# Store and load queues in a Fourier-mixing plus gated-ReLU kernel: slice stores on ScalarE's queue, plain copies on GpSimd's, down weights loaded sooner in fewer transfers

## The chip, the cores and the metric

One core of a Trainium2 chip runs the whole kernel. The metric is the device time of one launch, in microseconds, as the median of several runs. One further execution is recorded by the hardware profiler; the stretches and waits below are from that one.

## What is computed

```python
S, D, F = 2048, 640, 1728
xn = layernorm(x)                                  # x: (1, S, D), eps 1e-5, no scale or bias
a  = einsum("bsd,ed->bse", xn, dft_hid_re)         # DFT along the hidden dimension
b  = einsum("bsd,ed->bse", xn, dft_hid_im)
y  = einsum("ts,bse->bte", dft_seq_re, a) - einsum("ts,bse->bte", dft_seq_im, b)
gate, up = xn @ W_gate, xn @ W_up                  # (D, F)
h  = gate * (gate > 0) * up
out = x + y + h @ W_down                           # (F, D)
```

All arrays are float32.

## The kernel before

Every float32 operand of a matmul is written as a high and a low part (`split`: ScalarE copies to the rounded type, L197, VectorE subtracts, L198), and each product is three matmuls (`mm3`, L203 to L205). On top of that the products are arranged in Strassen-like schemes, so that VectorE and GpSimd make sums of operand blocks and TensorE does fewer multiplications. The kernel has three stages.

**The sequence transform** (to about 410 us of the profile). The sequence is cut in four chunks of 512 columns. For each chunk, units named B11, B21, T1, T2, B22, T3, T4, each four groups long, load 512 KB blocks of the sequence matrices (`raw`, six buffers; `tk`, four buffers that live from T1 to T4), subtract blocks where the name begins with T (L743), split them, and multiply them with the normalized rows, which stay on chip. `drive(4, 2)` runs the list of units: at step i it first runs what was deferred to step i, then prepares unit i-2, loads unit i, finishes i-5, and multiplies i-4. Loads are issued by SyncE. In this stage the engines' orders are left to the framework's scheduler, but for the instructions that are pinned.

Into this list go four *slices* (`token_slice`): for 128 columns out of each chunk, the transposed input is loaded (L472, five transfers of 256 KB) with the rows of means and roots (L474, two), normalized on VectorE (L479), and combined in 28 sums (L488, L490) that the gate/up stage will use as operands. The normalized blocks and the sums are stored to `tok` in HBM (L495, at most 7 blocks a transfer, 7 transfers a slice). `SLICE_PLAN` gives for each slice the unit at which it begins, the units of its four normalizing steps, the units of its sums, and the unit of its last stores. All slices use one tile, `r`.

**The gate/up stage** (about 410 to 760 us). 13 tiles of gate and up weights go through a written-out order: an event has a key in units of one `mm3`, a tile starts every 33 units (`PERIOD`), and all events are sorted by key and issued so on all five engines (`manual_schedule(engines=PINNED)`). `STEPS` holds the multiplications, seeds, snapshots, additions and results ("final") of a tile; `WEIGHTS` its weight splits; `SUMS` the sums of weight blocks. `plan_sums` places those sums beside VectorE's own PSUM work on GpSimd (L992, `sum_beside`) and, where a sum's due time has come, on VectorE. The weights of tile n are loaded at 33 n - `LOAD_LEAD` (L979, L984, L989) into buffers that the tile two before it used. Results go to `hd` in HBM with `store_final` (L1123). Operands 0 to 13 of the combined ones are loaded into their own tiles, later ones into the slots of operands that are done (`fill_slot`, L832); `split_slot` splits them `SPLIT_LEAD` units before their use.

In the same order stand the *down-weight tasks*: five `quad_weights` and 24 `pair_half`, three a tile from the third tile on. Each loads blocks of the hidden or down matrix into one of two `pw` tiles (pool `prep`; L1288, L1251, L1252), makes sums on VectorE (`prepare`), rounds them on ScalarE and VectorE (`round_`, `rounded`, L1270, L1305), and stores them to `wparts` or `wquads` (L1274, L1276, L1308). `TASK_KEYS` gives the key of `prepare` and of `rounded` for each of the three. The parts that need no sums are copied from HBM to HBM by `plain_parts` (L1236, L1237; 12 calls of four transfers). `grow` makes accumulating copies on GpSimd's queue (L1334, L1335).

**The down projection** (from about 760 us) multiplies `hd` and the first stage's results `pq` with `wparts` and `wquads`. Its units load rows (`rw`) and weights (`wt`), and `prepare` splits both.

SyncE issues nearly all transfers, in order: a transfer whose buffer or data is not ready holds those behind it. ScalarE issues a few at the start and the end. GpSimd issues `grow`, results of the sequence transform (`pq`, `first`) and outputs.

Of the kernel before, what the change touches and what calls it, by code (L numbers as in the profile page):

```python
# [7 lines left out]
F32 = mybir.dt.float32  # L8
# [4 lines left out]
P = 128  # L13
S, D, F = 2048, 640, 1728
KD = D // P
# [84 lines left out]
UPPER_ORDER = (2, 3, 5, 6, 7, 11, 4, 1, 0, 8, 9, 10, 12, 13)  # L100
NEV, STORED = 12, 10
LATE_LOW = 2
LEAD_ORDER = (2, 3, 5, 6, 7, 1, 0, 11, 8, 9, 10, 4, 13, 12, 5, 6)
LEADS = ((12, (24, 26)), (22, (34, 36)), (29, (40,)), (38, (45, 47)), (46.5, (52,)))
LEAD_SLOTS = (36, 37, 40, 41, 44, 45, 47, 49, 50, 51, 54, 55, 56, 57, 58, 59, 60, 61, 63, 64, 65, 66, 67, 68)
SPLIT_LEAD, FIRST_SPLIT = 6.5, -20
TASK_KEYS = ((5.2, 7.4), (14.6, 18.4), (29.7, 32.7))
LOAD_LEAD, LOADED = 48, 38
SLICE = P
# [16 lines left out]
def fnet_reglu_kernel(  # L126
# [329 lines left out]
    def token_slice(s):  # L456
# [9 lines left out]

        def load():
            if "work" not in late:
                late["work"] = get_r1(F32)
            t["w"] = late["work"]  # L470
            for k in range(KD):
                nc.sync.dma_start(by_chunk(at(k * NT, NT)), by_chunk(xt[k * P : (k + 1) * P])[:, :, cs])  # L472
            for i in range(2):
                nc.sync.dma_start(by_chunk(at(WORK_MR + i * NT, NT)), by_chunk(rows[i : i + 1])[:, :, cs].to_broadcast([P, NT, SLICE]))  # L474

# [15 lines left out]

        def store(first, at_, n):
            for i in range(0, n, 7):
                k = min(7, n - i)
                nc.sync.dma_start(tok[first + i : first + i + k, :, cs].rearrange("i p t -> p i t"), at(at_ + i, k).rearrange("p (i t) -> p i t", i=k))  # L495

        def begin():
            load()
            here, norms, units, end = SLICE_PLAN[s]
            for i, (k0, k1) in enumerate(((0, 2), (2, KD))):  # L500
                for m in range(2):
                    defer(norms[2 * i + m] - here, lambda m=m, k0=k0, k1=k1: normal(m, k0, k1))
            defer(norms[-1] + 1 - here, lambda: store(0, 0, NX))
            for i, part in enumerate(TOKEN_SUMS):
                defer(units[i * len(units) // len(TOKEN_SUMS)] - here, lambda part=part: sums(*part))
            defer(end - here, lambda: store(NX, WORK_OUT, NCOMBO))

# [374 lines left out]

    SLICE_PLAN = ((22, (26, 28, 29, 30), (30, 32, 33, 34, 39), 40), (40, (46, 48, 49, 50), (51, 53, 55, 56, 57), 58), (58, (67, 68, 69, 70), (72, 74, 77, 78), 79), (80, (88, 89, 90, 91), (93, 95, 98, 99), 100))
    SLICE_UNITS = [begin for begin, *_ in SLICE_PLAN]

# [113 lines left out]
    def plan_sums():  # L999
# [9 lines left out]
        def due_at(i):  # L1009
            if i not in due:  # L1010
                o = SUMS[i][1]
                raw = max(SUMS[i][3:]) >= ZR
                due[i] = min([split_at.get(o, 99.0) - 11, 2 * PERIOD - LOAD_LEAD - 1.0 if raw else 99.0] + [due_at(j) - 0.8 for j in reads.get(o, ())])
            return due[i]
# [117 lines left out]
    for n in range(NF):  # L1132
        k0 = PERIOD * n
        at(k0 - LOAD_LEAD if n > 1 else -70 + n * 30, load_tile, n)
        for key, *what in SUMS if n < 2 else ():
            at(max(k0 + key, 5 + key / 20) if n == 1 else k0 + key, sum_step, n, *what)
        for g, what in enumerate(WEIGHTS):
            at(k0 + what[0], high, n, g)
            at(k0 + what[0] + SPLIT_AHEAD, low, n, g)
        for key, what, *args in STEPS:  # L1140
            at(k0 + key, DO[what], n, *args)
            if what == "final":
                at(k0 + key + 2.2, store_final, n, args[0])

# [86 lines left out]
    def plain_parts(k):  # L1231

        wa, wb = pair(k, 1)
        for w, o1, o in ((wa[0], Y11, O1), (wb[0], Y12, O2)):
            rows = slice(0, w.shape[0])
            nc.sync.dma_start(wparts[rows, k, o1 : o1 + 2 * P], w[:, : 2 * P])  # L1236
            nc.sync.dma_start(wparts[rows, k, o : o + P], w[:, 2 * P : 3 * P])  # L1237

    def pair_half(k, h):
# [6 lines left out]
        def load():  # L1246
            t["z"] = z = pool("prep").tile([P, 12 * P], F32, name="pw")
            wa, wb = pair(k, 1)
            for w, o1, o2 in ((wa[0], y11, y21), (wb[0], y12, y22)):
                rows = slice(0, w.shape[0])  # L1250
                nc.sync.dma_start(z[rows, o1], w[:, h * P : (h + 1) * P])  # L1251
                nc.sync.dma_start(z[rows, o2], w[:, (3 + h) * P : (4 + h) * P])  # L1252

# [60 lines left out]
    for i, (load, prepare, round_, rounded, store) in enumerate(tasks):  # L1314
        key, second = (PERIOD * (2 + i // len(TASK_KEYS)) + key for key in TASK_KEYS[i % len(TASK_KEYS)])
        at(key - 7, load)
        at(key, prepare)
        at(key + 1.2, round_)
        at(second, rounded)
        at(second + 1.5, store)  # L1320
    for k in range(NPAIR):
        at(30 + 8 * k, plain_parts, k)

# [126 lines left out]
    def project(q):  # L1450
# [27 lines left out]
        def unit(name, u, first, last):  # L1478
# [42 lines left out]
            def prepare():  # L1521
# [18 lines left out]
                with in_turn():  # L1540
# [19 lines left out]
                    t["b"] = b = pool("ring2").tile([P, 2, SG, CH], F32R, name="cb")[:, :, :n]  # L1560
                    lows.append(split(b[:, 0], b[:, 1], src))
                    if name not in PARTS:
                        w = t["w"]
                        split(w[:, :, 0], w[:, :, 1], w[:, :, 1].bitcast(F32))

# [215 lines left out]
```

## Time and profile before

| | us |
|---|---|
| median of 3 runs | 1036.5 (1036.24 to 1039.34) |
| profiled execution, device time | 1042.62 |
| its span, first to last instruction | 1040.8 |
| TensorE busy | 1008.0 (97%) |
| VectorE busy | 886.1 (85%) |
| ScalarE busy | 526.7 (51%) |
| GpSimd busy | 120.5 (12%) |

The page gives busy time by engine, the span in slices, DMA queues, the chain of work that ended last, groups of instructions, and DMA issues. In its rows PE is TensorE's matmuls, PEld its weight loads, DVE VectorE, ACT ScalarE, POOL GpSimd and SP SyncE; a q behind an engine's name is its queue. `raw<-in_dft` is what an instruction writes and reads, buffer numbers left out; L743 is a line of the kernel. Sequencer work such as issuing a DMA is not counted as busy. A wait is put down to the event that ended it.

### The profile page before, as it was taken

Reading aid. Unit: us, or ns where it says so; the run is one execution under the profiler, and the core shown is the slowest. Engines: PE = TensorE matmul, PEld = TensorE weight load, DVE = VectorE, ACT = ScalarE, POOL = GpSimd, SP = SyncE. Lnnn points to the kernel's source line nnn. Section 1 sums busy time; section 2 is a strip of 40 time slices with the busy share of each in tenths; the row PEclk is TensorE's granted clock in tenths of the full one; section 3 lists DMA queues with packets and bytes.
Section 4 is the critical chain, followed back from the end, with each engine's and each line's share of the span. In section 5 each row is a group of like instructions: output and inputs, shape, how many; then the busy total and the mean of one; then the engine's idle time right before and its main releaser. Section 6 shows DMA issues by size and latency. Waiting matters only on the chain.

```text
span 1040.8 us, 13595 instructions
## 1 busy us (share of the span) xinstructions
PE 1008.0 (97%) x4393; PEld 825.4 (79%) x4393; DVE 886.1 (85%) x1442; ACT 526.7 (51%) x832; POOL 120.5 (12%) x235
## 2 busy tenths in 40 slices
PE   9999999899999999999899989999999999999998
PEld 8888888688788888777778768778878888888887
DVE  7969999888889989997889879897878888599887
ACT  6654443223233555675566556666534554454552
POOL 2000000000000000022323323322000000000001
PEclk9999999999999999999899999999999999999999
DMA  9887895965958858749867978753689688999685
GB/s 333 327 252 241 278 316 180 365 205 191 345 181 298 318 182 257 270 140 255 243 197 218 213 210 228 208 167 120 199 331 359 215 260 296 321 314 346 209 273 178
DMA packets 189319, 261.14 MB, mean 251 GB/s; under 512 B 15712, under 2 KB 133984, under 8 KB 189152
## 3 DMA queue, kind: packets, MB, share of 16 engines
q1 hardware_dynamic: 179776, 226.03, 65.6%
q0 software_dynamic: 9040, 33.82, 10.9%
q8 instruction: 34, 0.56, 0.2%
q10 hardware_dynamic: 432, 0.43, 0.1%
q14 instruction: 37, 0.30, 0.1%
HBM read 198.34 MB, written 75.94 MB: 264 GB/s over the span
## 4 chain that ended last, share of the span: by engine, by line
PE 62%; DVE 20%; DMA 10%; ACT 3%; issue 3%; SPq 2%; POOL 0%; DVEq 0%; ACTq 0%; POOLq 0%
PE ps L203 19%; PE ps L204 19%; PE ps L205 19%; DVE cb L198 4%; PE ps L576 3%; DMA wparts<-pw 2%; DMA tk<-in_dft 2%; DVE raw L743 2%; DMA hd<-ev 1%; DMA pw<-in_wd 1%; DVE ev L1102 1%; DVE r L490 1%; DVE gw L992 1%; DMA pw<-in_hid 1%; DVE tk L743 1%
## 5 line engine op out<-in xcount | busy, mean ns | idle before, releaser
L203 PE MATMUL ps<-cb,wt 128*128 128x512 f32 (+1 forms) x389 | 151.5, 389 | 1.2 <-ACT cb L197 1.2
L204 PE MATMUL ps<-cb,wt 128*128 128x512 f32 (+1 forms) x389 | 151.8, 390 | 0.8 <-DVE cb L198 0.8
L205 PE MATMUL ps<-cb,wt 128*128 128x512 f32 (+1 forms) x389 | 151.4, 389 | 0.0
L197 ACT ACTIVATE cb<-rw 128x1024 fp32r<-128x1024 f32 (+1 forms) x91 | 86.5, 962 | 79.5 <-PE ps L205 40.6
L197 ACT ACTIVATE cb<-raw 128x1024 fp32r<-128x1024 f32 x64 | 67.8, 1061 | 106.9 <-PE ps L205 76.5
L198 DVE TENSOR_TENSOR cb<-rw,cb 128x1024 fp32r<-128x1024 f32 (+1 forms) x91 | 99.5, 1104 | 21.4 <-ACT cb L197 20.8
L204 PE MATMUL ps<-cb,xs_late 128*128 128x512 f32 x232 | 92.4, 398 | 7.7 <-DVE cb L198 7.7
L1087 ACT ACTIVATE ps<-ps 128x512 f32<-128x512 f32 x104 | 60.2, 582 | 71.4 <-DVE ps L1097 43.3
L205 PE MATMUL ps<-cb,xs_late 128*128 128x512 f32 x232 | 91.8, 396 | 0.0
L198 DVE TENSOR_TENSOR cb<-raw,cb 128x1024 fp32r<-128x1024 f32 x64 | 77.9, 1220 | 16.3 <-ACT cb L197 16.0
L203 PE MATMUL ps<-cb,xs_late 128*128 128x512 f32 x232 | 91.5, 394 | 0.0
L204 PE MATMUL ps<-cb,xs_early 128*128 128x512 f32 x226 | 88.3, 391 | 0.0
L203 PE MATMUL ps<-cb,xs_early 128*128 128x512 f32 x226 | 88.2, 390 | 0.0
L205 PE MATMUL ps<-cb,xs_early 128*128 128x512 f32 x226 | 88.2, 390 | 0.0
L203 PEld LDWEIGHTS ps<-cb,wt 128*128 128x128 f32 x389 | 73.4, 189 | 16.8 <-ACT cb L197 1.6
L204 PEld LDWEIGHTS ps<-cb,wt 128*128 128x128 f32 x389 | 73.4, 189 | 16.1 <-DVE cb L198 1.1
L205 PEld LDWEIGHTS ps<-cb,wt 128*128 128x128 f32 x389 | 73.5, 189 | 15.2
L194 ACT ACTIVATE ev<-ps 128x512 f32<-128x512 f32 x117 | 68.8, 593 | 24.7 <-PE ps L205 22.1
L1102 DVE TENSOR_TENSOR ev<-ps,ev 128x512 f32<-128x512 f32 x91 | 62.3, 685 | 9.2 <-PE ps L205 8.8
L197 ACT ACTIVATE wt<-wt 128x768 fp32r<-128x768 f32 (+5 forms) x60 | 38.4, 645 | 53.7 <-DMA wt<-wparts 50.1
L197 ACT ACTIVATE cb<-tk 128x1024 fp32r<-128x1024 f32 x32 | 33.9, 1061 | 61.0 <-PE ps L205 27.3
L203 PE MATMUL ps<-mv,w 128*128 128x512 f32 x143 | 57.2, 400 | 7.7 <-ACT ps L1087 7.6
(248 smaller groups left out, 2283.8 us busy)
## 6 DMA issues: line engine op xcount, KB each, us to landing
raw<-in_dft SPq DMA_DIRECT2D x94, 512.0 KB, 6.3
wt<-wparts SPq DMA_DIRECT2D x74, 256.0 KB, 4.7
rw<-hd SPq DMA_DIRECT2D x27, 512.0 KB, 6.2
hd<-ev SPq DMA_DIRECT2D x45, 256.0 KB, 3.6
tok<-r SPq DMA_DIRECT2D x24, 448.0 KB, 5.1
wt<-wparts SPq DMA_DIRECT2D x27, 384.0 KB, 4.3
rw<-pq SPq DMA_DIRECT2D x19, 512.0 KB, 5.7
wparts<-pw SPq DMA_DIRECT2D x24, 384.0 KB, 3.5
```

What stands on the lines that cost most here:

```text
L194: return nc.scalar.activation(o, i, AF.Copy)
L197: nc.scalar.activation(hi, src, AF.Copy)
L198: return nc.vector.tensor_tensor(lo, src, hi.bitcast(F32), op=OP.subtract)
L203: nc.tensor.matmul(ps, wh, mh, start=first, stop=False, skip_group_check=more)
L204: nc.tensor.matmul(ps, wh, ml, start=False, stop=False, skip_group_check=more)
L205: nc.tensor.matmul(ps, wl, mh, start=False, stop=last, skip_group_check=more)
L490: pin(tt(two(o[0], o[3]), two(o[1], o[4]), two(o[2], o[5]), op=op))
L576: nc.tensor.matmul(E[0, key], xn_part(n * SG + j, d)[v == 1], b[:, int(v == 2), j], start=False, stop=n % NH == NH - 1 and (j, v) == (SG - ...
L743: sub = lambda o, i0, i1: nc.vector.tensor_tensor(o, i0, i1, op=OP.subtract)
L992: return (engine or nc.vector).tensor_tensor(operand(n, o), operand(n, a), operand(n, b), op=OP.add if op == "+" else OP.subtract)
L1087: nc.scalar.activation(banks[n, x], banks[n, s], AF.Copy, scale=float(sign))
L1102: tt(t, banks[n, x], snaps[n, s], op=OP.add if op == "+" else OP.subtract)
```

## The change

- Slice stores (L495) are issued by ScalarE instead of SyncE, and each of the three or four transfers has a step of its own. A slice's seven loads are spread over steps 0 to 4 behind its begin (`SLICE_LOADS`), its last stores over 1 and 2 steps behind the planned end (`SLICE_STORES`). `SLICE_PLAN` is new; slice 2 begins at 62 instead of 58, slice 3 at 81 instead of 80.
- The plain copies are issued by GpSimd, one every 6 units from key 66 on, instead of four at a time every 8 units from key 30 on by SyncE.
- A down-weight task's load comes 9.5 units before `prepare` instead of 7, its store 3 units after `rounded` instead of 1.5; `pair_half` loads in two transfers instead of four; `TASK_KEYS` is new.
- A gate/up tile is loaded 46 instead of 48 units ahead, and sums of raw blocks are due at 11.5 instead of 17.
- A result's store comes 4 units after it instead of 2.2 (and its buffer counts as used for 11 instead of 10); operand splits come 5.5 units before their use instead of 6.5, and the first at -16 instead of -20.
- In the down projection, T1's weight split of the first half is issued after the ScalarE copy of the last B11 rows.

```diff
-NEV, STORED = 12, 10
+NEV, STORED, STORE_LAG = 12, 11, 4
...
-SPLIT_LEAD, FIRST_SPLIT = 6.5, -20
-TASK_KEYS = ((5.2, 7.4), (14.6, 18.4), (29.7, 32.7))
-LOAD_LEAD, LOADED = 48, 38
+SPLIT_LEAD, FIRST_SPLIT = 5.5, -16
+TASK_LEAD, TASK_KEYS = 9.5, ((8.2, 12.4), (14.6, 18.4), (28.0, 29.9))
+LOAD_LEAD, LOADED, RAW_DUE = 46, 38, 11.5
+SLICE_LOADS, SLICE_STORES = (0, 1, 2, 3, 3, 4, 4), (1, 1, 2, 2)
...
-        def store(first, at_, n):
-            for i in range(0, n, 7):
-                k = min(7, n - i)
-                nc.sync.dma_start(tok[first + i : first + i + k, :, cs].rearrange("i p t -> p i t"), at(at_ + i, k).rearrange("p (i t) -> p i t", i=k))
+        def store(first, at_, i, n):
+            k = min(7, n - i)
+            nc.scalar.dma_start(tok[first + i : first + i + k, :, cs].rearrange("i p t -> p i t"), at(at_ + i, k).rearrange("p (i t) -> p i t", i=k))
 
         def begin():
-            load()
             here, norms, units, end = SLICE_PLAN[s]
+            for unit, f in zip(SLICE_LOADS, [lambda k=k: load(k) for k in range(2)] + [lambda i=i: load_rows(i) for i in range(2)] + [lambda k=k: load(k) for k in range(2, KD)]):
+                if unit:
+                    defer(unit, f)
+                else:
+                    f()
...
-            defer(norms[-1] + 1 - here, lambda: store(0, 0, NX))
+            for i in range(0, NX, 7):
+                defer(norms[-1] + 1 + i // 7 - here, lambda i=i: store(0, 0, i, NX))
...
-            defer(end - here, lambda: store(NX, WORK_OUT, NCOMBO))
+            for i in range(0, NCOMBO, 7):
+                defer(end + SLICE_STORES[i // 7] - here, lambda i=i: store(NX, WORK_OUT, i, NCOMBO))
...
-    SLICE_PLAN = ((22, (26, 28, 29, 30), (30, 32, 33, 34, 39), 40), (40, (46, 48, 49, 50), (51, 53, 55, 56, 57), 58), (58, (67, 68, 69, 70), (72, 74, 77, 78), 79), (80, (88, 89, 90, 91), (93, 95, 98, 99), 100))
+    SLICE_PLAN = ((22, (26, 28, 28, 29), (30, 33, 33, 35, 39), 40), (40, (46, 49, 50, 52), (52, 53, 55, 55, 57), 58), (62, (66, 67, 69, 70), (72, 74, 77, 77), 81), (81, (88, 89, 90, 93), (93, 95, 98, 99), 100))
...
-                due[i] = min([split_at.get(o, 99.0) - 11, 2 * PERIOD - LOAD_LEAD - 1.0 if raw else 99.0] + [due_at(j) - 0.8 for j in reads.get(o, ())])
+                due[i] = min([split_at.get(o, 99.0) - 11, RAW_DUE if raw else 99.0] + [due_at(j) - 0.8 for j in reads.get(o, ())])
...
-                at(k0 + key + 2.2, store_final, n, args[0])
+                at(k0 + key + STORE_LAG, store_final, n, args[0])
...
-        for w, o1, o in ((wa[0], Y11, O1), (wb[0], Y12, O2)):
-            rows = slice(0, w.shape[0])
-            nc.sync.dma_start(wparts[rows, k, o1 : o1 + 2 * P], w[:, : 2 * P])
-            nc.sync.dma_start(wparts[rows, k, o : o + P], w[:, 2 * P : 3 * P])
+        return [lambda w=w, o=o, c=c: nc.gpsimd.dma_start(wparts[: w.shape[0], k, o : o + (c.stop - c.start)], w[:, c])
+                for w, o1, o in ((wa[0], Y11, O1), (wb[0], Y12, O2)) for o, c in ((o1, slice(0, 2 * P)), (o, slice(2 * P, 3 * P)))]
...
-            for w, o1, o2 in ((wa[0], y11, y21), (wb[0], y12, y22)):
-                rows = slice(0, w.shape[0])
-                nc.sync.dma_start(z[rows, o1], w[:, h * P : (h + 1) * P])
-                nc.sync.dma_start(z[rows, o2], w[:, (3 + h) * P : (4 + h) * P])
+            blocks = z.rearrange("p (o n) -> p o n", n=P)
+            for w, put in ((wa[0], slice(2, 5, 2)), (wb[0], slice(3, 11, 7))):
+                nc.sync.dma_start(blocks[: w.shape[0], put], w.rearrange("p (o n) -> p o n", n=P)[:, h : h + 4 : 3])
...
-        at(key - 7, load)
+        at(key - TASK_LEAD, load)
...
-        at(second + 1.5, store)
-    for k in range(NPAIR):
-        at(30 + 8 * k, plain_parts, k)
+        at(second + 3, store)
+    for i, f in enumerate(f for k in range(NPAIR) for f in plain_parts(k)):
+        at(2 * PERIOD + 6 * i, f)
...
+                    if name == "B11":
+                        late["copied"] = next(i for i in reversed(nc.cur_bb.bb.instructions) if i.engine == mybir.EngineType.Activation)
                     if name not in PARTS:
                         w = t["w"]
-                        split(w[:, :, 0], w[:, :, 1], w[:, :, 1].bitcast(F32))
+                        with tc.issue_after(late["copied"]) if (q, name) == (1, "T1") else ExitStack():
+                            split(w[:, :, 0], w[:, :, 1], w[:, :, 1].bitcast(F32))
```

More of the change, by code (lines that the diff above doesn't have):

```diff
@@ L465, in at, with load @@
             return t["w"][:, o * SLICE : (o + n) * SLICE]
-        def load():
+        def load(k):
             if "work" not in late:
@@ L470, in load, with load_rows @@
             t["w"] = late["work"]
[L471 to L474, printed above, removed]
+            nc.sync.dma_start(by_chunk(at(k * NT, NT)), by_chunk(xt[k * P : (k + 1) * P])[:, :, cs])
+        def load_rows(i):
+            nc.sync.dma_start(by_chunk(at(WORK_MR + i * NT, NT)), by_chunk(rows[i : i + 1])[:, :, cs].to_broadcast([P, NT, SLICE]))
         def normal(m, k0, k1):
```

## The prediction

> **What bounds the kernel now.** I read the page's first part, then the table of stretches, TensorE's waits, and for each stretch that loses time the queue or the chain of work in it. TensorE is the bound: it is busy for 97% of the span, so what can be gained is where it stands still, and the half clock that follows.
>
> ```profile
> span 1040.8 us, 13595 instructions
> 200.00:212.00 12.00, 6.82 (x18) 5.04 (x17) 9.04 (x10) 3.17 (x3) 0.14 (x1) 0.72 0.99 397
> 212.00:273.00 61.00, 61.00 (x271) 50.46 (x270) 53.05 (x64) 19.91 (x20) 2.55 (x5) 1.00 0.67 218
> 273.00:281.00 8.00, 5.46 (x18) 4.10 (x17) 6.71 (x6) 1.46 (x2) 0.00 (x0) 0.79 1.03 420
> 412.00:490.00 78.00, 74.65 (x321) 59.21 (x320) 70.75 (x161) 54.03 (x107) 14.79 (x30) 1.00 0.72 219
> 490.00:530.00 40.00, 33.40 (x133) 26.36 (x132) 29.01 (x67) 20.69 (x42) 9.16 (x18) 0.91 0.84 249
> 570.00:615.00 45.00, 38.53 (x160) 30.39 (x159) 35.03 (x82) 25.55 (x52) 14.74 (x27) 0.96 0.90 222
> 615.00:665.00 50.00, 49.88 (x219) 40.63 (x218) 45.00 (x103) 31.76 (x63) 17.70 (x36) 1.00 0.78 212
> 665.00:710.00 45.00, 43.51 (x190) 34.99 (x189) 40.45 (x97) 28.75 (x58) 11.93 (x25) 1.00 0.57 167
> 760.00:769.00 9.00, 7.03 (x24) 5.16 (x23) 6.55 (x7) 3.99 (x5) 0.54 (x1) 0.81 0.98 362
> 769.00:1025.00 256.00, 256.00 (x1131) 211.97 (x1130) 213.17 (x252) 121.81 (x157) 8.47 (x16) 1.00 0.87 293
> ```
>
> Behind each stretch stand its length, then busy time and count of TensorE, weight loads, VectorE, ScalarE and GpSimd, the granted clock, the DMA engines' busy share and GB/s. The last row is TensorE undisturbed: 256.00 us for 1131 matmuls, 0.2263 us each. Length minus count times 0.2263 is what a stretch loses:
>
> - A, 200 to 212: 7.9 us. B, 273 to 281: 3.9. Both in the sequence transform.
> - C, 412 to 490, where the gate/up stage starts: 5.4.
> - D, 490 to 530: 9.9; 570 to 615: 8.8; 615 to 665: 0.4; 665 to 710: 2.0; together 21.1, inside the gate/up stage.
> - E, 760 to 769, at the start of the down projection: 3.6.
>
> In all 42.0 us, clock loss included (in A, 12 us at 0.72 lose 3.4 to the clock alone). 615 to 665 says more: there VectorE and ScalarE do the whole of their gate/up work, and TensorE runs at full rate. So D is no lack of VectorE, it is lateness.
>
> Why A and B are late, from SyncE's queue, VectorE and the chain of work in order of time (start, length, what):
>
> ```profile
> 177.87 3.80 SPq L495 DMA_DIRECT2D tok<-r  x4
> 181.71 4.14 SPq L472 DMA_DIRECT2D r<-in_xt  x4
> 185.90 2.30 SPq L474 DMA_DIRECT2D r<-rows  x2
> 185.77 2.35 DVE L743 TENSOR_TENSOR raw<-raw,tk 128x1024 f32<-128x1024 f32 x2
> 191.58 11.58 DMA tk<-in_dft
> 203.25 1.23 DVE L743 TENSOR_TENSOR tk<-tk,raw 128x1024 f32<-128x1024 f32 x1 [2.50 <-DMA tk<-in_dft]
> PE ps L204 <- DVE cb L198: 8.5, 3, 5.2
> 251.50 4.55 SPq L495 DMA_DIRECT2D tok<-r  x4
> 256.09 4.67 SPq L472 DMA_DIRECT2D r<-in_xt  x4
> 265.19 9.00 DMA tk<-in_dft
> ```
>
> From 177.87 to 188.20 SyncE's queue does nothing but store one slice's sums (L495) and load the next slice (L472, L474). The matrix tile that T1 of the next chunk needs (tk) could have been asked for at 188.12, when the two L743 subtractions that free its buffers are done; it is asked for at 191.58, behind other late loads, and takes 11.58 us. VectorE stops in front of its subtraction, the low half that TensorE wants next stands behind that in VectorE's order, and TensorE idles 5.2 us. B is the same picture one chunk later.
>
> Why D is late, from SyncE's waits in the gate/up stage, its queue there, and the chain:
>
> ```profile
> SPq L984 <- DVE gw L992: 28.3, 6, 6.4
> SPq L1276 <- DVE pw L1270: 21.0, 16, 3.0
> SPq L979 <- DVE gw L992: 15.9, 4, 5.4
> SPq L1251 <- DMA wparts<-pw: 14.4, 12, 4.1
> 583.25 0.35 SPq L984 DMA_DIRECT2D gw<-in_wgu  x1
> 587.28 5.36 DMA pw<-in_hid
> 596.29 6.61 DMA wparts<-pw
> wparts<-pw SPq DMA_DIRECT2D x24, 384.0 KB, 3.5
> L1236 SPq DMA_DIRECT2D wparts<-in_wd x14: 496/605/1636, 468.2 to 513.3; - x14
> 483.66 8.44 DMA wparts<-in_wd
> ```
>
> (Total us, times, longest.) One queue carries everything: the gate/up tile load waits until a VectorE sum has read the old tile (L984, L979), the down-weight store waits for its rounding (L1276), the next down-weight load waits for a buffer (L1251). Loads of pw stand behind all of these, so they land as VectorE reaches their prepare step, or later: at 587.28 the load takes 5.36 us more, and VectorE, in order, holds up the sums on which ScalarE's seeds and TensorE hang. At 483.66 the plain copies wparts<-in_wd add 8.44 us in front of a pw load.
>
> **The change part by part.** One unit of the gate/up order is three matmuls, 0.68 us.
>
> *Slice stores on ScalarE, slice transfers spread (A, B).* The 28 stores leave SyncE; slice 2 begins at unit 62 instead of 58, its seven transfers at 62 to 66 instead of all at once, stores one or two units after the sums. In A, tk's second load can then go at 188.12, 3.5 us sooner, and four of the seven transfers (256 KB each) go behind it, at 397 GB/s another 2.6 us: landing near 197.1 instead of 203.16. TensorE needs 5.2 us, so the idle time goes; VectorE has no slack there, so I leave 0.8 us. A: -7.1. In B the slice begins at 81 instead of 80 and its stores move from 79 to 82 and 83, so the same bytes still meet T1's loads. tk is again freed earlier than it is asked for, but I count only half of the 2.5 us of idle time as gone, with the clock loss (8 us at 0.79, 1.7 us): 1.4 remain. B: -2.5.
>
> What the stores cost on ScalarE:
>
> ```profile
> L495 SPq DMA_DIRECT2D tok<-r x28: 365/512/2040, 100.7 to 322.9; - x28
> SPq L495 <- DVE r L479: 34.3, 8, 8.8
> L197 ACT ACTIVATE cb<-raw 128x1024 fp32r<-128x1024 f32 x64 | 67.8, 1061 | 106.9 <-PE ps L205 76.5
> ```
>
> The issues take 512 ns in the median (365 to 2040), 14 us for 28, on an engine that is busy 19.91 us of 61 and whose high-half copies (cb<-raw) wait 76.5 us for TensorE to free a buffer. I take +0.5, between 0 and what the third rival says.
>
> *Gate/up loads and down weights (D).* The raw sums' due time goes from 17.0 (2 x 33 - 48 - 1) to 11.5, and the tile load from key 18 to 20; walking the planner's rule through with both, one raw sum of each tile moves, and it stays on VectorE. So the load no longer finds its buffer read late. The rounding's store comes 3 units after it, not 1.5; a final's store 4 after it, not 2.2. The down-weight load leads by 9.5 units instead of 7, in two transfers instead of four. The third task of a tile: its load stood behind the tile load and the second task's store (VectorE's key 18.4); with about 2 us of issue and 5.36 us to land it came at key 29.4, wanted at 29.7. Now it is keyed 18.5, ahead of both, and waits only for the first task's store: rounding at 12.4, 3.5 us to land by the row of its kind (to key 17.6 to 18.5, counting issue), then 3 to 5.4 us: key 23 to 26.5, wanted at 28.0. That is 1 to 3 us of slack in place of none. The 48 plain copies leave SyncE (0.6 us each in front of pw loads) and go one per 6 units. I take 70% of D away: -14.8; the rest covers landings like the 6.61 us above and late seeds, which stay.
>
> ```profile
> L1334 POOL DMA_DIRECT2D grown<-grown x6 | 3.3, 547 | 5.2 <-DMA grown<-hd 4.8 <-DMA grown<-pq 0.4
> DVE gw L992 <- POOL gw L992: 2.2, 3, 1.8
> ```
>
> The copies cost GpSimd 48 x 0.55 = 26 us, on an engine with two thirds of its time free (14.74 of 45 busy). What can be late is its sums: VectorE waited 2.2 us for them beside 24 such DMAs. Twice as many: 4.4 at most, 0 at least; I take +1.5, between the two and nearer to the row's own 2.2.
>
> *Start of the gate/up stage (C).* Splits move 4 and 1 units later, giving VectorE room first and less lead after. The trace has no row for either; 0, plus or minus 2.
>
> *The order at the down projection (E).* T1's weight split is held behind ScalarE's copy of B11.
>
> ```profile
> 758.48 3.33 DMA wt<-wparts
> 761.90 0.84 ACT L197 ACTIVATE wt<-wt 128x768 fp32r<-128x768 f32 x1 [7.32 <-DMA wt<-wparts]
> 762.65 1.99 ACT L197 ACTIVATE cb<-rw 128x1024 fp32r<-128x1024 f32 x2
> ```
>
> ScalarE sat idle 7.32 us for T1's weights and only then copied B11's rows, for which TensorE was waiting. With the copies first, E goes but for about 0.7: -2.9 (0 if their buffers are not free sooner).
>
> Sum: -7.1 - 2.5 + 0.5 - 14.8 + 1.5 - 2.9 = -25.3 on the profiled execution, whose own time is 1042.6 (span 1040.8): 1017.3. The median of the runs, 1036.5, is 6.1 shorter. I take it that those 6.1 are of the same stalls, so scale by (42.0 - 6.1)/42.0 = 0.855: -21.6, 1014.9.
>
> **The rivals.**
>
> 1. *The DMA engines, not the queue, are full.* At 200 to 212 they are 0.99 busy, at 273 to 281 1.03. If the same bytes land as late, A and B stay: -25.3 + 9.6 = -15.7, times 0.855 is -13.4, 1023. Against it: 212 to 273 ran at 0.67, so there is room before B, and in A the queue stood waiting for VectorE first. The Trainium skill, "DMA: Bandwidth & Descriptors", section "Issuing engines are not separate DMA queues", says that DMAs of all issuing engines run on the same 16 engines and that another issuer saves sequencer time only; by that rule it is this rival that holds. The trace agrees inside A (397 GB/s), and shows with L495's 34.3 us of waits that a queue can hold transfers back for another reason.
> 2. *The down-weight buffers hold the queue.* There are two; a store that comes 1.5 units later frees its buffer later, and the third load, keyed 18.5, waits on SyncE in front of the tile load. If D gives a third (-7.0): -17.5, times 0.855 is -15.0, 1021.5. With the first rival too: 1030.
> 3. *ScalarE stops for the slices* (the other side). SyncE stood 34.3 us for L479 in front of L495. If ScalarE stands as long, each time with a cb copy behind it that TensorE wants, that is up to +34.3, less the 0.5 already counted, some 1049. It decides from 21.6, two thirds of those waits: from there the kernel is slower. Against it: SyncE runs ahead of VectorE and ScalarE does not, since its copies wait for VectorE's subtractions or TensorE's buffers, and the store comes a unit after its data.
> 4. *No change*, each stall replaced by the next late thing: 1036.
>
> **How the numbers follow.** Forecast 52% (its own spread about 1005 to 1021), rival 1 18%, rival 2 19%, both 2%, rival 3 6%, no change 3%. 0.3%, 3.1 us, is about what a measurement can tell. Faster 0.91, same 0.03, slower 0.06. Low end: all of A, B, D and E (36.5 times 0.855 is 31.2) and 2 of C, 1003; I stop at 1004. High end: both rivals, 1030.
>
> **What the changed profile would show.** Right: no wait for cb of over 2 us near 200 and 273, tk landing within 8 us of its issue; no half clock between 490 and 615; L984 and L979 waits below 10 us in sum; ScalarE copying cb before its third wt at the down projection. Wrong: ScalarE waiting for r before L197 (rival 3), SyncE's wait for wparts<-pw above 14.4 us (rival 2), tk still 9 to 12 us on its way (rival 1), VectorE waiting for GpSimd's sums by more than 5 us, or new gaps at C.

## The result, and the profile after

The changed kernel is faster, by about half to four fifths of the forecast gain.

| | changed, us | before, us | ratio, 95% interval |
|---|---|---|---|
| first comparison | 1026.27 (1024.63 to 1026.56, 4 runs) | 1037.05 (1036.24 to 1039.34) | 0.9889 [0.987, 0.9909] |
| second comparison, another chip | 1024.49 (1024.26 to 1025.15, 4 runs) | 1042.08 (1039.99 to 1045.72, 11 runs) | 0.983 [0.9813, 0.9848] |

The two intervals do not meet. Between them the changed kernel moved by 1.8 us and the kernel before by 5.0; in the other two groups of runs below the kernel before stood at 1041.19 and 1040.56. So the gain is 10.8 us or 17.6, and most of the difference is in the kernel before. What makes the kernel before vary so was not found. The profiled executions were 1042.6 before (span 1040.8), 1026.4 and 1024.3 after (spans 1024.6 and 1022.5).

The table of stretches, first of the kernel before and then of the changed one. The borders are the starts of TensorE's matmuls number 800, 1100, 1300, 1800, 2100, 2600, 3100 and 3500 (of 4393), so each pair of rows is the same work; the third row of each, 500 undisturbed matmuls, is left out. The columns are length, TensorE's busy time (count), granted clock, busy share of the DMA engines, GB/s.

```profile
177.54:254.04 76.50, 71.32 (x301) 0.96 0.73 249
254.04:303.84 49.80, 47.26 (x201) 0.97 0.88 309
...
417.17:490.77 73.60, 70.25 (x301) 1.00 0.71 212
490.77:624.04 133.27, 120.20 (x501) 0.96 0.79 221
624.04:740.45 116.41, 114.81 (x501) 1.00 0.62 179
740.45:835.78 95.33, 93.07 (x401) 0.98 0.82 286
```

```profile
177.70:250.32 72.62, 70.14 (x301) 0.98 0.78 264
250.32:298.55 48.23, 46.18 (x201) 1.00 0.84 308
...
411.88:484.33 72.45, 70.27 (x301) 1.00 0.60 183
484.33:608.66 124.33, 115.95 (x501) 1.00 0.87 246
608.66:725.37 116.71, 115.34 (x501) 1.00 0.65 188
725.37:819.53 94.16, 92.50 (x401) 1.00 0.84 289
```

A, the first row, is 3.9 us shorter, B 1.6, C 1.2, D (two rows) 249.7 to 241.0, 8.6, and E 1.2. At 0.2263 us a matmul the lengths would be 67.9, 45.3, 67.9, 226.3 and 90.5: A still loses 4.7 us, D 14.7.

**What is left in A**, from the changed kernel. The stores of a slice (L495) between 177 and 207 (issue ns min/median/max, first and last start):

```profile
L495 ACTq DMA_DIRECT2D tok<-r x4: 366/370/521, 177.9 to 185.1; - x4
DMA to landing us min/median/max: 5.0/9.1/20.0
```

SyncE's queue by the timeline (start, length, line), the landing of the four `tk` loads between 180 and 212, the waits of SyncE and TensorE, and the last step of the chain of work:

```profile
177.91 1.25 SPq L472 DMA_DIRECT2D r<-in_xt  x2
179.20 3.15 SPq L475 DMA_DIRECT2D r<-rows  x2
182.40 1.93 SPq L472 DMA_DIRECT2D r<-in_xt  x2
...
187.05 1.46 SPq L753 DMA_DIRECT2D tk<-in_dft  x2
...
194.06 11.46 SPq L753 DMA_DIRECT2D raw<-in_dft  x2
205.60 0.38 SPq L753 DMA_DIRECT2D tk<-in_dft  x1
```

```profile
DMA to landing us min/median/max: 4.8/10.9/11.1
```

```profile
SPq L753 <- DMA tok<-r: 12.8, 4, 10.5
PE ps L205 <- DVE cb L199: 2.5, 1, 2.5
```

```profile
205.60 4.84 DMA tk<-in_dft
```

The store issued at 185.1 lands after 20.0 us, at 205.1, and until then SyncE stands in front of a load: 10.5 us, the 11.46 of its two issues. That load does not touch `r`. By the trace's semaphore events the transfers of SyncE and ScalarE take turns on eight completion semaphores, and an issue waits until the earlier transfer on its semaphore has landed; this load's was the store's. Only then is the fourth tk asked for (205.60); it lands quickly (4.84), but late, and TensorE idles 2.5 us. So the stores left SyncE's queue and still hold it. The first lines show a second thing: with no store in front of them, six of the slice's seven loads (the first went at 169.94) are issued in one go from 177.91 to 184.3, all of them before the first tk (187.05). The spread of the loads is gone from the queue, and three of the four tk loads take 10.7 to 11.1 us.

**What is left in D**: SyncE's waits, those of VectorE, TensorE and GpSimd, and two pieces of the chain.

```profile
SPq L1255 <- DMA wparts<-pw: 69.4, 24, 5.9
SPq L1291 <- DMA wquads<-pw: 10.5, 3, 5.5
SPq L985 <- DVE wb L1074: 7.5, 2, 7.1
SPq L990 <- DVE gw L998: 3.3, 1, 3.3
PE ps L204 <- DVE ev L1108: 8.0, 5, 3.2
DVE gw L998 <- POOL gw L998: 6.5, 5, 3.0
POOL grown L1337 <- DMA grown<-hd: 7.4, 1, 7.4
```

```profile
483.84 7.76 DMA wquads<-pw
492.05 5.72 DMA pw<-in_wd
...
580.49 9.93 DMA grown<-hd
590.76 4.07 DMA grown<-grown
```

The waits that D was made of before, of tile loads for a sum (`gw`), are down from 44.2 us to 3.3; a wait for a weight split (`wb`) is 7.5, before 3.7. In their place SyncE waits 69.4 us (51.6 in the second profile) for down-weight stores to land, since a task's load needs the tile that the store still reads. At 483.84 a store takes 7.76 us, the next load goes at 492.05 and takes 5.72, and TensorE stands 3.2 us near 497. The second piece is GpSimd's queue: an accumulating copy (`grown<-hd`) takes 9.93 us to land, and GpSimd waits 7.4 us of them before it issues the copy of its result (`grown<-grown`, 4.07), for which the next accumulating copy waits in turn. GpSimd's sums stand behind, and VectorE (6.5 us) behind them.

### The profile page after: what moved, and what is told of

It is laid out like the page before. It is cut to its first block, busy times and chain, and to the rows that moved or that the text cites. A ratio compares the mean times of both kernels' runs of the same rounds, so it can differ in the third digit from the quotient of the medians.

```text
span 1024.6 us, 13553 instructions
## 1 busy us (share of the span) xinstructions
PE 1001.7 (98%) x4393; PEld 817.9 (80%) x4393; DVE 884.8 (86%) x1442; ACT 525.7 (51%) x832; POOL 145.7 (14%) x283
## 4 chain that ended last, share of the span: by engine, by line
PE 69%; DVE 16%; DMA 9%; issue 3%; ACT 2%; POOL 1%; SPq 1%; DVEq 0%; ACTq 0%; POOLq 0%
PE ps L204 21%; PE ps L205 21%; PE ps L206 21%; DVE cb L199 3%; PE ps L582 3%; DMA raw<-in_dft 2%; DVE r L491 2%; DMA wparts<-pw 1%; DVE tk L749 1%; DMA pw<-in_wd 1%; DMA grown<-hd 1%; DMA r<-in_xt 1%; DVE ev L1108 1%; PE ps L611 1%; DVE r L480 1%
## 5 line engine op out<-in xcount | busy, mean ns | idle before, releaser
L205 PE MATMUL ps<-cb,xs_late 128*128 128x512 f32 x232 | 90.5, 390 | 2.1 <-DVE cb L199 2.1
L206 PE MATMUL ps<-cb,xs_late 128*128 128x512 f32 x232 | 90.3, 389 | 0.0
L204 PE MATMUL ps<-cb,xs_late 128*128 128x512 f32 x232 | 90.3, 389 | 0.0
L1093 ACT ACTIVATE ps<-ps 128x512 f32<-128x512 f32 x104 | 59.3, 581 | 56.0 <-PE ps L206 28.8
L206 PEld LDWEIGHTS ps<-cb,wt 128*128 128x128 f32 x389 | 73.0, 188 | 14.7
L195 ACT ACTIVATE ev<-ps 128x512 f32<-128x512 f32 x117 | 69.1, 595 | 22.5 <-PE ps L206 20.6
L998 POOL TENSOR_TENSOR gw<-gw 128x128 f32<-128x128 f32 x97 | 47.6, 491 | 126.6 <-DVE gw L998 39.9
```

Source lines behind the costliest of these rows:

```text
L195: return nc.scalar.activation(o, i, AF.Copy)
L204: nc.tensor.matmul(ps, wh, mh, start=first, stop=False, skip_group_check=more)
L205: nc.tensor.matmul(ps, wh, ml, start=False, stop=False, skip_group_check=more)
L206: nc.tensor.matmul(ps, wl, mh, start=False, stop=last, skip_group_check=more)
L998: return (engine or nc.vector).tensor_tensor(operand(n, o), operand(n, a), operand(n, b), op=OP.add if op == "+" else OP.subtract)
L1093: nc.scalar.activation(banks[n, x], banks[n, s], AF.Copy, scale=float(sign))
```

## Experiments

Each was timed beside runs of the kernel before on the same chip. Letters for theories are those of the expectation that they stand in. The lengths below are of the stretches above, from the profile of each kernel, worked out in the same way. D1 and D2 in the expectations are what the first and the second row of D lose against 0.2263 us a matmul; the kernel before was timed in four groups of runs.

| kernel | median, us | ratio, 95% interval | A | B | C | D | E |
|---|---|---|---|---|---|---|---|
| before | 1037.05, 1041.19, 1040.56, 1042.08 | | 76.5 | 49.8 | 73.6 | 249.7 | 95.3 |
| changed, first profile | 1026.27 | 0.9889 [0.987, 0.9909] | 72.6 | 48.2 | 72.5 | 241.0 | 94.2 |
| changed, second profile | 1024.49 | 0.983 [0.9813, 0.9848] | 70.4 | 48.3 | 72.8 | 239.6 | 94.9 |
| slice part alone | 1032.71 | 0.992 [0.9903, 0.9938] | 69.6 | 48.2 | 72.7 | 251.4 | 95.1 |
| slice part, stores on SyncE | 1031.88 | 0.9902 [0.9881, 0.9924] | 68.4 | 46.1 | 72.7 | 248.4 | 94.9 |
| gate/up part alone | 1039.22 | 0.9987 [0.997, 1.0004] | 75.5 | 48.6 | 76.9 | 242.7 | 95.2 |
| plain copies alone | 1038.99 | 0.9974 [0.9953, 0.9996] | 75.5 | 52.2 | 74.7 | 246.5 | 94.3 |
| projection order alone | 1040.62 | 1.0002 [0.9982, 1.0022] | 75.9 | 49.7 | 72.7 | 248.2 | 94.1 |
| changed, stores on SyncE | 1020.95 | 0.9812 [0.9789, 0.9835] | 68.4 | 46.0 | 72.7 | 239.5 | 93.8 |
| changed, stores on GpSimd | 1036.19 | 0.9958 [0.9933, 0.9983] | 69.3 | 45.3 | 72.7 | 246.1 | 94.0 |
| changed, free stores | 1022.73 | 0.9826 [0.9804, 0.9848] | 69.8 | 48.1 | 72.5 | 239.5 | 94.2 |
| changed, grow 15 apart | 1029.81 | 0.9893 [0.9865, 0.992] | 69.6 | 48.2 | 72.9 | 245.7 | 94.0 |
| both of these | 1015.83 | 0.975 [0.9728, 0.9772] | 74.1 | 48.2 | 73.3 | 231.6 | 94.0 |
| candidate | 1033.26 | 0.9915 [0.9899, 0.993] | 68.4 | 46.2 | 73.1 | 255.6 | 94.1 |

How far one profile can be read: before, slice part, slice part with stores on SyncE, and projection order have the same plan in D, and their D is 248.2 to 251.4. Below 3 us in D, and 1 us in C and E, nothing is concluded from one of them. Nor is the profiled execution the median one: it is the slowest of its kernel's runs for the slice part (1034.62), the stores on GpSimd (1041.43), both causes of D away (1019.41) and the candidate (1035.0), and the fastest for the slice part with stores on SyncE (1028.34), the changed kernel with them (1018.36) and the gate/up part (1036.66).

### Each part alone on the kernel before

The slice part: the new `load`, `store` and `SLICE_PLAN`, nothing else.

> The kernel before with the slice part alone (stores on ScalarE, transfers spread, the new slice plan). Theory A (the parts add up as the two profiles' stretches show): the sequence transform gave 5.6 us of the profiled gain of 16.2, so 1031 to 1033 us, 4 to 6 below the kernel before. Rival B (stores on ScalarE hold SyncE's loads back through the completion slots that both queues share, so that little is left): 1036 to 1037, at most 1 us of gain.

The gate/up part: the constants, `RAW_DUE`, `STORE_LAG`, `TASK_LEAD`, the store 3 units after `rounded`, the two-transfer loads; the plain copies as before.

> The kernel before with the gate/up timing alone: due times, load leads, fewer down-weight transfers, later stores and splits; the plain copies stay on SyncE, four at a time from key 30 on. Theory A: half or more of the gate/up gain of 9.9 us in the profiles, so 1031 to 1033. Rival C (the two down-weight buffers hold SyncE's queue, so the earlier leads gain nothing without the copies' move): 1035 to 1038.

The plain copies:

```diff
-    for k in range(NPAIR):
-        at(30 + 8 * k, plain_parts, k)
+    for i, f in enumerate(f for k in range(NPAIR) for f in plain_parts(k)):
+        at(2 * PERIOD + 6 * i, f)          # and nc.gpsimd instead of nc.sync in plain_parts
```

> The kernel before with the plain copies alone moved to GpSimd, one every 6 units. Theory A: the stall near 490 us was theirs (9.9 us lost between 490 and 530 in the profile before), so 1030 to 1034. Rival D (GpSimd's sums come late behind copies and accumulating transfers): 1036 to 1039, with VectorE waiting over 5 us for GpSimd's sums.

The order at the down projection:

```diff
+                        with tc.issue_after(late["copied"]) if (q, name) == (1, "T1") else ExitStack():
```

> The kernel before with the order of ScalarE's copies at the start of the down projection alone. Theory A: 3.2 us gained at the start, 2 given back since transfers there come at the DMA engines' rate: 1035 to 1036, about 1 us. Rival E (nothing is given back): 1033 to 1034.

The medians beside 1041.19 are -8.5, -2.0, -2.2 and -0.6 us: together -13.2, inside the 10.8 to 17.6 of the whole. The slice part is the only large one. The expectations were worked out from the first group's 1037: as gains, theory A's 4 to 6 us for the slice part were too few, the gate/up part and the plain copies stay below theory A's 4 and 3, and the order alone is told neither from theory A's 1 us nor from none. With the plain copies VectorE waits 3.3 us for GpSimd's sums, not the over 5 of rival D. The gate/up part shortens D by 7.0 us in its profile and gains 2.0 in the median, which its own interval does not tell from none; which of its constants shortens D was not tried apart. Its waits, then its stretches for C and D:

```profile
SPq L1251 <- DMA wparts<-pw: 53.2, 21, 6.1
```

```profile
414.97:491.83 76.86, 71.25 (x301) 0.98 0.72 218
491.83:619.54 127.71, 120.07 (x501) 0.97 0.81 222
619.54:734.52 114.98, 114.56 (x501) 1.00 0.63 181
```

The wait for the stores' landing comes from this part (53.2 us; with the plain copies alone it is 14.3 at the same load, before 14.4). And C is 3.3 us longer than before, which it is not in the whole change (72.5, 72.8) nor, beyond noise, with the plain copies alone (74.7). This suggests, from one profile each, that this part needs the plain copies out of SyncE's queue.

### The queue of the slice stores

One word in L495 of the changed kernel:

```diff
-            nc.scalar.dma_start(tok[first + i : first + i + k, :, cs]...
+            nc.sync.dma_start(tok[first + i : first + i + k, :, cs]...     # or nc.gpsimd
```

> The changed kernel with the slice stores back on SyncE's queue, all else of the slice part kept (spread, plan). Theory U (SyncE's waits for slice data in front of the stores, 34.3 us before, were the loss; the queue is what matters): A and B lose 10 us or more in the profile, ratio to the kernel before 0.992 to 0.996. Rival V (spreading the transfers and beginning slice 2 later was what mattered): A and B as in the changed kernel or less, ratio 0.987 to 0.990.

> The changed kernel with the slice stores on GpSimd's queue instead of ScalarE's. Theory S (in the changed kernel a store on ScalarE's queue that lands late, up to 20.0 us, holds one of eight completion slots that SyncE's loads use too; GpSimd's transfers have eight of their own): no SyncE wait for a tok store, losses of A and B together at most 5 us in the profile instead of 7.7, time 1 to 3 us below the changed kernel, a ratio to the kernel before of 0.986 to 0.988. Rival T (the DMA engines are full there whoever asks): A and B lose 7 to 8, ratio 0.988 to 0.991.

On SyncE it is the fastest of the kernels here that leave nothing out, 1020.95, and A and B together are within 1.2 us of undisturbed. Theory U failed. Rival V's lengths held, and the ratio is better than its 0.987. On GpSimd A and B are short too (1.4 us lost), as theory S has it, but its ratio, 0.9958, is worse than both theories', for a new stall stands earlier; from that kernel's waits and the chain:

```profile
ACT sb L195 <- DMA pq<-sb: 13.7, 2, 12.7
PE ps L204 <- ACT sb L195: 7.7, 1, 7.7
```

```profile
155.27 8.25 DMA pq<-sb
```

GpSimd stores the transform's results (`pq`); a slice store waiting for its data in front of one of these keeps `sb` occupied, ScalarE waits 12.7 us for it, and TensorE 7.7. That is not all of the loss: the stretch between B and C takes 119.20 us there instead of 113.33, and D is 246.1; these two were not followed up.

Then the slice part alone again, on the kernel before, with its stores left on SyncE; and in the same group the changed kernel once more.

> The kernel before with the slice part of the change alone, the stores left on SyncE's queue: loads and stores one at a time, spread over the steps, and the new plan of slices. With the stores on ScalarE's queue this part alone stood at 0.992 [0.9903, 0.9938]. Q: faster than that, about 0.985 (1025 where the kernel before stands at 1040), with A and B at about 1 us each instead of 1.8 and 3.0. O: the same 0.992 (1032). By both D1 keeps its 19 to 20 us, since the plan of the down-weight preparation is that of before.

> The changed kernel once more, unchanged, on the same chip and beside the same runs of the kernel before as the three kernels sent with it. Both theories (Q: the slice stores' move to ScalarE's queue costs time; O: it costs nothing by itself, and the variant with the stores on SyncE gained by another order on VectorE and by the chip it ran on) expect about 0.989 of the kernel before, 1027 to 1030 where the kernel before stands at 1040. In its profile the slice store issued near 185 lands after more than 12 us and SyncE's next load waits for it, if that is a trait of the program; it lands in about 5 if the 20 us of the first profile were a single event. D1 loses about 10 us again.

Of the slice part with stores on SyncE: SyncE's wait, the landing of the stores from 177 to 207, its queue near A (some lines left out), the landing of tk, and stretches A and B.

```profile
SPq L495 <- DVE r L480: 32.9, 8, 7.4
```

```profile
DMA to landing us min/median/max: 4.3/6.1/6.7
```

```profile
177.85 4.12 SPq L495 DMA_DIRECT2D tok<-r  x4
...
183.19 1.23 SPq L472 DMA_DIRECT2D r<-in_xt  x2
...
187.00 0.33 SPq L753 DMA_DIRECT2D tk<-in_dft  x1
187.38 0.48 SPq L475 DMA_DIRECT2D r<-rows  x1
```

```profile
DMA to landing us min/median/max: 8.4/8.7/8.9
```

```profile
177.26:245.64 68.38, 68.30 (x301) 1.00 0.80 279
245.64:291.75 46.11, 45.69 (x201) 1.00 0.90 327
```

SyncE waits as long for the slices' normalized rows as in the kernel before (32.9 against 34.3), and A and B are free of stalls: those waits cost nothing. The four stores still go in one go here (177.85, 4.12 us). What differs from the kernel before is the loads behind them: there six followed at once (181.71 to 188.20), ahead of the first tk; here four of the seven go behind the first tk (187.38 to 195.41), and tk lands in 8.4 to 8.9 us, before in 9.8 to 12.4. Whether the spread of the loads does this or the new `SLICE_PLAN`, by which slice 2 begins at 62, was not tried apart. With the stores on ScalarE the slowest of the four in A took 14.4 to 21.5 us to land in all six profiles that have them there, with SyncE the slowest took 5.4 to 6.7 in the four that were looked at (the kernel before among them). The six have A and B at 117.8 to 122.3 together, the three of the new slice plan with the stores on SyncE at 114.4 to 114.6.

Theory Q is half borne out. The profiles say 3 to 8 us in A and B. The times say less: 0.9902 against 0.992, 0.9812 against 0.983, both with intervals that overlap; in medians 0.8 us and 3.5 to 5.3. That the kernels with the stores on ScalarE lose more in A and B is shown, its size in the whole time is open within 0 to 5 us. What of it is the queue itself is not shown: with the one word changed, the scheduler also chose another order on VectorE in this stage, and in SyncE's queue it put all of slice 2's loads ahead of tk. Those orders were not held fixed in any run. The 10.5 us that SyncE stands for a store's landing are read from the trace; in the slice part alone that wait is 3.8.

### The two causes in D

Free stores: the stores of prepared sums read the gate/up weights in HBM (`wgu`, an input of the kernel and not a tile, as the third expectation below calls it), so no load waits for the tile that a store reads. It leaves out that the prepared sums reach device memory.

```diff
-                                z[:, : 2 * P].rearrange("p (a n) -> p a n", a=2))
+                                wgu[0][:, : 2 * P].rearrange("p (a n) -> p a n", a=2))   # and so for the other two
```

> The changed kernel with the down-weight tasks' stores reading gate/up weights in HBM instead of the task's tile, same sizes and times: it leaves out that the prepared sums reach HBM, and the two tiles come free with the rounding, not with the landing. Theory C (the two tiles hold SyncE's queue: 69.4 us of waits for wparts<-pw in the changed kernel): those waits go, the gate/up stage loses 4 to 8 us in the profile instead of 11.8, ratio 0.982 to 0.986. Rival D (GpSimd's late sums are what is left): the gate/up stage loses 10 to 12, ratio 0.988 to 0.990.

GpSimd's accumulating copies further apart:

```diff
-            at(key + 9 * i, step)
+            at(key + 15 * i, step)
```

> The changed kernel with the steps of the accumulating copies 15 units apart instead of 9, so that GpSimd does not stand for a copy that has not landed (7.4 us near 583 in the changed kernel) with its sums behind it. Theory D (GpSimd's late sums are part of the loss left in the gate/up stage): GpSimd waits for no copy of its own, VectorE waits under 3 us for its sums instead of 6.5, 2 to 4 us gained, ratio 0.985 to 0.987. Rival C: no more than 1 us, ratio 0.988 to 0.990.

Both together (the output again lacks the prepared sums):

> The changed kernel with both suspected causes in D taken away at once: the stores of the prepared sums read the gate/up tile instead of the prepared tile, so that no load of plain down weights waits for the tile that a store still reads (it leaves out that the prepared sums reach device memory), and the steps that GpSimd's sums grow in stand 15 matmul steps apart instead of 9. Theory V (two causes stand behind one another in D, each covering the other): D1 falls from 10 to 3 to 6 us and the time to about 1018 to 1021 where the changed kernel stands at 1027 to 1030, with VectorE's wait for GpSimd's sums below 2 us. Rival W (a third thing, such as the full transfer engines or VectorE's own order, sets D1): D1 stays near 10 and the time within 2 us of that with the free stores alone (0.9826 of the kernel before).

VectorE's wait for GpSimd's sums, in the kernel with free stores and then in the one with wider steps:

```profile
DVE gw L998 <- POOL gw L998: 10.0, 6, 2.9
```

```profile
DVE gw L998 <- POOL gw L998: 0.9, 2, 0.6
```

Stretch D of the kernel with both:

```profile
487.05:603.11 116.06, 115.06 (x501) 1.00 0.88 250
603.11:718.60 115.49, 114.58 (x501) 1.00 0.71 204
```

With the first alone SyncE's waits for those stores are gone and D stays as it was (239.5), while GpSimd is now waited for 10.0 us. So rival D is nearer by the lengths; its ratio, 0.9826, is in theory C's range, but the changed kernel itself stood at 0.983 in the second comparison. With the second alone that wait is 0.9 and D is no shorter than in the changed kernel (245.7, SyncE's wait at L1255 82.7 us). There theory D failed: the wait went and no time with it. With both D falls to 231.6, 5.3 above undisturbed, and the time to 1015.83, below the 1018 to 1021 expected, though this profile has the slowest A of all the variants of the changed kernel. So D had two causes and either alone was enough to keep most of it. Full transfer engines, the third thing of rival W, do not set D: over its first row they are 0.88 busy in the kernel with both and 0.87 in the changed one, 8 us longer.

### A candidate

Stores on SyncE, growing steps 15 apart, and the task stores early, to free the tile sooner:

```diff
-TASK_LEAD, TASK_KEYS = 9.5, ((8.2, 12.4), (14.6, 18.4), (28.0, 29.9))
+TASK_LEAD, TASK_KEYS = 9.5, ((8.2, 10.4), (14.6, 16.8), (28.0, 29.9))
...
-        at(second + 3, store)
+        at(second + 0.5, store)
```

> A candidate to beat both: the changed kernel with the slice stores on SyncE's queue, the task stores at second + 0.5 with earlier second halves, and the growing steps 15 apart. Q and V together: A and B below 1 us each as with the stores on SyncE, D1 down to 4 to 7 us, 1014 to 1018 where the kernel before stands at 1040 (0.975 to 0.979). By O and W: about 1026 to 1030, like the changed kernel. If the earlier task steps put VectorE's work in D in the way of TensorE's operands, D2 rises above 4 us and it ends at about 1020 to 1023.

It missed: A and B are as short as they should be, D is the longest of all, 255.6.

```profile
SPq L1277 <- DVE pw L1265: 68.2, 23, 5.2
DVE pw L1262 <- DMA pw<-in_wd: 14.3, 4, 5.1
DVE pw L1262 <- DMA pw<-in_hid: 11.7, 4, 6.0
PE ps L204 <- ACT ps L1093: 15.4, 12, 3.5
```

The store now reaches SyncE's queue before VectorE is done with its data: SyncE stands 68.2 us there (3.9 in the changed kernel), the loads behind it are late, VectorE waits 14.3 + 11.7 us for them, and ScalarE's seeds (L1093) come late for TensorE. The wait for the landing (11.7 us at L1255 instead of 69.4) was traded for a worse one. The earlier rounding and the earlier store were not tried apart.

## Why the prediction was right, and where its size was wrong

The direction and the range held: 1026.3 and 1024.5 lie within 1004 to 1030, the likeliest value 1015 is about 10 us too low. By its steps, on the profiled executions:

- *A and B, -7.1 and -2.5, and +0.5 for the issues on ScalarE.* Measured -3.9 and -1.6, in the second profile -6.1 and -1.5. The step that failed is "four of the seven transfers go behind it". With the stores gone from SyncE's queue tk's second load did go at 188.18, as forecast (188.12), but all seven slice loads were ahead of it, it landed at 199.2 instead of 197.1, and the fourth tk had to wait for a store's landing. With the stores kept on SyncE four of the seven do go behind the first tk, and A and B fall by 11.8 (126.3 to 114.5), more than forecast; the kernels with the stores on ScalarE give 3.3 to 7.8 of it back. The term that I priced at +0.5, by the issue time, belongs here: the issues did stay cheap (367 ns in the median of 28), but their landing holds SyncE through the shared completion semaphores, which I had not looked for.
- *D, -14.8 with +1.5 for GpSimd's copies.* Net measured -8.6 and -10.1 against -13.3. The tile loads' waits went as the prediction said (L979 and L984 there, L985 and L990 here, 44.2 us for a sum to 3.3, or 47.9 to 10.8 with those for a split). What came instead was its second rival's wait, and its own sign for it: 69.4 us where 14.4 was the limit. The step that failed is the slack of the third task. The prediction counts the landing from the rounding at key 12.4 and leaves out that the store comes 3 units later, as it says itself in the same paragraph: the tile is free at key 20.6 to 21.5, not 17.6 to 18.5, and the load, keyed 18.5, stands in front of the others until then. By its own prices the data then come at key 25 to 29.4, wanted at 28.0: from 2 us early to 1 us late, not 1 to 3 early. The stores also land later than the 3.5 us of that sum, in 4.4 and 4.7 us in the median (L1277, L1279). How much of the 69.4 us each of these makes was not tried apart. The +1.5 was taken as VectorE waiting longer for GpSimd; that wait rose from 2.2 to 6.5, over the bound of 4.4 and the mark of 5. The bound counted GpSimd's copies; in the piece followed above, the wait comes from accumulating copies behind one another's landing. GpSimd waits 15.4 us for such copies instead of 10.1, though each takes little longer to land (5.9 us in the median instead of 5.6).
- *C, 0 plus or minus 2.* -1.2 and -0.8.
- *E, -2.9.* -1.2 and -0.5, and alone the order gave nothing that the runs can tell (1.0002). TensorE's wait for ScalarE fell from 1.2 us to 0.2 and the half clock behind it went, as said; TensorE's waits for VectorE's low halves there did not.
- *The scaling by 0.855.* It rested on a median of three runs, 1036.5. The kernel before stood at 1040.6 to 1042.1 in three later groups, so the profiled 1042.6 was an ordinary time, and the step that put the stalls 6.1 us lower was unfounded. Against 1042.6 the unscaled 1017.3 compares with 1026.4 and 1024.3. (The five losses add up to 41.9, not 42.0, which changes nothing.)

Rival 1 (full DMA engines) had its own sign: three of the four tk loads in A were still 10.7 to 11.1 us on their way. But full engines need not stall TensorE. With the stores on SyncE A has no stall, though they are 1.05 busy from 178 to 206 (in the changed kernel 0.95, before 1.01) and 0.80 and 0.90 over the whole of A and B. What differs is the order of what they carry. The Trainium skill, "DMA: Bandwidth & Descriptors", section "Issuing engines are not separate DMA queues", says that another issuer saves only the sequencer's time and that the transfers interleave. That the move would bring little by itself agrees: 1024.5 and 1026.3 against 1020.95 with the stores back on SyncE. That stores on the other queue could land in 20.0 instead of 6.7 us is not in it. Rival 2 (the buffers hold the queue) came true in mechanism, and its time, 1021.5, was nearer than the forecast; in part by luck, for it takes all of the gain in A and B and a third of D's loss, and the runs gave less of the first (5.5 and 7.6 us of 9.6) and more of the second (8.6 and 10.1 us net, not 5.5). Rival 3 (ScalarE stops for the slices) fell: ScalarE's largest waits for slice rows in the changed kernel are 1.7 and 1.3 us. The half clock between 490 and 615 was gone in the first profile (1.00) and came back in part in the second: 0.97 over its first stretch of D.

## What to carry to other kernels

Where the loads of a slice went behind the transfers that TensorE needed first, the stall was gone, though the queue waited as long as before. Moving the stores to another engine's queue brought the loads back in front, and a wait for the stores' landing: before moving, look up what an issue waits for and what moves up behind it, not only what it costs. When two late things stand at one stall, an experiment that removes one can show nothing; remove both before calling either harmless. And a store asked for before its data is ready holds everything behind it on that queue (68.2 us of waits in the candidate), so earlier is not always better.

## What the runs showed of the hardware

The slowest of four slice stores of 448 KB landed in 5.4 to 6.7 us in this place when the queue that issued the loads also issued them, and in 14.4 to 21.5 us when ScalarE issued them beside SyncE's loads, six profiles of six. Why was not settled: in those six the slice loads also go out in one go beside the stores (177.91 to 184.3 in the changed kernel), and a second queue was not tried with the loads in the other order.

The half clock did not follow a fixed length of idle time. In the 14 profiled executions TensorE's granted clock fell to half for 3.4 us or 6.8 us after every gap of 3.5 us and more, after some from 1.1 to 3.4 us (one of 1.95 was enough in the kernel with the stores on GpSimd) and not after others (2.68 and 3.19 in the changed kernel's first profile, 3.39 in the slice part alone). The Trainium skill, "TensorE: Matmul & The Clock Gate", section "Part 1: The HAM clock gate (the "warmup" mystery)", puts the idle window at about 3.4 us and calls it free-running; the runs agree with the 3.4 us of half clock and show that shorter gaps can be enough, so that a stall's price is uncertain by 1.7 us (half of 3.4) or more.
